# A block of sliding-window attention, mixer and MLP: modulation sums and the output projection's chain listed later, unit 0 packed over two queues, and a unit's products with V in one burst in place of two

## Chip, cores and metric

The kernel runs on one core of a Trainium2 chip. The metric is the device time of one execution in microseconds (us). Engines are named as in the profile: PE (TensorE, matmul), DVE (VectorE), ACT (ScalarE), POOL (GpSimd) and SP (SyncE, which here only issues DMAs).

## The reference

One batch of S = 2048 rows, D = 576 columns, H = 32 heads of 18, a window of W = 256, all in float32:

```python
mod = (_silu(c) @ w_mod).reshape(c.shape[0], 6, 1, -1)       # sa, ca, ga, sb, cb, gb
h = _layernorm(x) * (1 + ca) + sa
x = x + ga * _A_ref(h, A_wqkv, A_wo)      # attention: causal, 256 keys per query, then @ wo
h = _layernorm(x) * (1 + cb) + sb
x = x + gb * _B_ref(h, B_w1, B_w2, B_w3, B_w4)
# _B_ref: x1 = x + shift(gelu(ln(x) @ w1)) @ w2;  x1 + gelu(ln(x1) @ w3) @ w4   (w3: 576 x 4608)
```

## The kernel before

Each float32 operand of a matmul is split in a high and a low part, and products are taken from both, so one product of the reference is two or three matmuls. Phase A does the first layer norm, the projections to q, k and v, the attention, and most of the output projection; phase B/C does the mixer and the MLP, with weights and rows that flow through PE without a list.

**Attention.** It is cut in 32 units (c, g, hq): four chunks c of eight heads, four groups g of 512 rows, two halves hq of four heads. Names of tiles carry these numbers: `X0_3_0_1_2` is c 0, g 3, hq 0, bank 1 (of 128 query rows' windows), head 2. A unit's steps are:

- `uload` (L444 to L460): twelve DMAs on SP copy the q and k parts of the unit from DRAM (`qkh`, `qkl`) into the tile `U`, of which there are four.
- `s2` (L464 to L503): 16 score matmuls `sc` on PE (L477, three PSUM buffers), each reduced to a row maximum by DVE (L484). Then DVE negates and splits the maxima into `mr` (L490, L491), PE transposes them (`mT`, L498), ACT copies them out as `ms` (L500) and sends them by a DMA from its own queue (L501) into two rows of `U`, so that the next matmuls subtract the maximum by themselves.
- `s3` (L505 to L581): matmuls `X` (L526), which need those two rows, with a mask added by PE (L527, three PSUM buffers), exponential on ACT into `P` (L533, four buffers of four heads), and the products of P with V, `av` (L548): matmuls of 128 x 32 columns, four heads side by side in the PE array. They come in bursts: banks 0 and 3 in a burst in mid-unit, banks 1 and 2 in a burst at the unit's end. Then `fin1` copies the sums out on ACT (L553), `fin2` transposes and divides them (`oT`, L560, L562, `o`, L566), and `fin3` stores `o` from SP (`od`, L570) when hq is 1.

The X of a unit run 1.5 unit-times behind its scores, so that X of one unit and scores of the next but one alternate on PE. 

**Order.** Phase A's steps are put in a list `ev` of (time, step), with one unit per unit-time, and `play` (L40) calls them in the order of time. PE, POOL and SP keep that order (`manual`, L1192); DVE and ACT get theirs from the scheduler. An engine executes its instructions in order, so an instruction that waits holds up all behind it. SP's transfers also take turns on eight completion lanes, with ACT's: a transfer waits until the one before it on its lane has landed.

**Modulation vectors.** `modvec(v)` (L186 to L221) makes one of the vectors 2 to 5 beside the attention: five loads of rows of `w_mod` on SP (L196), products and sums on POOL (L205, L207, L208), then `spill`: PE adds over partitions with a matrix of ones (`pm`, L215), DVE reads it back (L216), and SP stores the vector (L219). L719 to L724 give these steps their times: `t0 = shift + 7.0 + 2.8 * n`, loads at `t0 + 0.35 * k`, spill at `t0 + 2.2`, store at `t0 + 2.35`.

**Output projection.** `s4(g, i)` (L736 to L785) handles one of 16 tiles of 128 rows: SP loads the tile of `o` back (`or`, L743) and the rows of x (L745); PE transposes it and ACT and DVE split it (`oTT`, L64 to L74); two halves of 14 matmuls each give `po` (L763), DVE adds x (L764), SP stores it (L769), and DVE makes the two layer norms that follow, whose results SP stores too. Times within a tile come from `d4` (load, transpose, half 0, half 1, norm, norm), and tiles of groups 0 to 2 are placed in the attention of the last chunk; group 3's follow it in phase B/C.

Of the kernel before, what the change touches and what calls it, by code (L numbers as in the profile page):

```python
# [19 lines left out]
P = 128  # L20
# [5 lines left out]
DH = 18  # L26
CH = 8
NCH = H // CH
SCALE = DH ** -0.5
# [21 lines left out]
class Kern:  # L51
# [75 lines left out]
    def phase_a(self):  # L127
        nc = self.nc
# [10 lines left out]
        with ExitStack() as st:  # L139
            self.ps = self.pool(st, "psA", space=PSUM)  # L140
            wp = self.pool(st, "wA")
            rp, lp, row = self.rp, self.lp, self.row
            pp = self.pool(st, "pA")
            V = [wp.tile([P, H * VA + 13], F32, name=f"V{t}") for t in range(NT)]
# [285 lines left out]
            def ualloc(n):  # L430
                def f():
                    pool, tag, nb = (lp, "L", 4) if n < 3 else (pp, "W", 1)
                    u = pool.tile([P, 4 * 512 + 2 * 768], F32R, tag=tag, name=f"U{n}", bufs=nb)
                    q = u[:, 0:2048].rearrange("p (q n) -> p q n", q=4)
                    k = u[:, 2048:].rearrange("p (j n) -> p j n", j=2)
                    nc.gpsimd.memset(k.bitcast(F32), 1.0)
                    nc.gpsimd.memset(q.bitcast(F32), 0.0)
                    units.append((q, k))
                return f

# [3 lines left out]
            def uload(c, g, hq):  # L444
                def f():
                    q, k = unit(c, g, hq)
                    h0 = 8 * c + 4 * hq

                    def put(dst, row, src, first, r, c0, c1):
                        v = src[first:first + 4 * DH, c0:c1].rearrange("(j r d) n -> d j r n", r=2, d=DH)[:, :, r, :]  # L450
                        nc.sync.dma_start(dst[row:row + DH].bitcast(F32), v)

                    c0, c1 = max(0, g * 512 - 256), g * 512 + 512
                    kd = k[:, :, 768 - (c1 - c0):]
                    for r in range(2):
                        for n, src in enumerate((qkl, qkh, qkh)):
                            put(kd, 64 * r + n * DH, src, D + h0 * DH, r, c0, c1)
                        for n, src in enumerate((qkh, qkh, qkl)):
                            put(q[:, r::2, :], 64 * r + n * DH, src, h0 * DH, r, g * 512, c1)
                return f  # L460

            KR = P - 2
# [42 lines left out]
            def s3(c, g, hq):  # L505
                QZ, KZ = unit(c, g, hq)
                Pb, Xb, abox = {}, {}, []
                banks = [0, 3, 1, 2] if g else [3, 1, 2]

                def sc(b, q):  # L510
                    def f():
                        if q == 0:
                            Pb[b] = pp.tile([P, 4, 3 * P], F32, tag="P", name=f"P{c}_{g}_{hq}_{b}", bufs=self.b_p)
                        j = q // 2
                        X = self.ps.tile([P, 3, P], F32, tag="st", name=f"X{c}_{g}_{hq}_{b}_{q}", bufs=self.b_st)
                        if b == 0:
                            mms = [(0, 1, 0, 0), (1, 2, 1, 0)]
                            mk = maskb[:, 1, :].unsqueeze(1).to_broadcast([P, 2, P])
                        elif b < 3:
                            mms = [(0, 3, b + 1, b - 1)]  # L520
                            mk = maskb
                        else:
                            mms = [(0, 2, 4, 2), (2, 1, 5, 3)]
                            mk = maskb[:, 0, :].unsqueeze(1).to_broadcast([P, 2, P])
                        for n, (x0, nb, kb, qb) in enumerate(mms):
                            nc.tensor.matmul(X[:, x0:x0 + nb, :].rearrange("p a b -> p (a b)"), KZ[:, j, kb * P:(kb + 1) * P], QZ[:, q, qb * P:(qb + nb) * P], start=(n == 0), stop=False)  # L526
                        nc.tensor.matmul(X[:, 0::2, :], self.identb, mk, start=False, stop=True)  # L527
                        Xb[b, q] = X
                    return f

                def expo(b, q):
                    def f():
                        nc.scalar.activation(Pb[b][:, q, :], Xb[b, q].rearrange("p a b -> p (a b)"), AF.Exp, scale=SCALE)  # L533
                    return f

                def av(b):
                    def f():
                        if not abox:
                            abox.append(self.ps.tile([P, 512], F32, tag="av", name=f"av{c}_{g}_{hq}", bufs=self.b_av))
                        first = b == banks[0]  # L540
                        segs = {0: [(-1, 0, 2 * P, P), (-2, 0, P, 0)],
                                1: [(0, 0, 3 * P, 0)] if g else [(0, 0, 2 * P, 0), (0, 2 * P, P, 2 * P)],
                                2: [(1, P, 3 * P, 0)],
                                3: [(2, 2 * P, 2 * P, 0), (3, 3 * P, P, 2 * P)]}[b]
                        for n, (kb, q0, w, p0) in enumerate(segs):
                            for q in range(4):
                                hv = (8 * c + 4 * hq + q) * VA
                                nc.tensor.matmul(abox[0][32 * q:32 * q + 32, q0:q0 + w], V[4 * g + kb][:, hv:hv + 32], Pb[b][:, q, p0:p0 + w], start=(first and n == 0), stop=(b == banks[-1]))  # L548
                    return f

                def fin1():
# [20 lines left out]
                steps = []  # L572
                n = 0
                for k, b in enumerate(banks):
                    for q in range(4):
                        steps += [(n, sc(b, q)), (n + self.l_e, expo(b, q))]
                        n += 1
                    if (len(banks) - k) % 2:
                        for b2 in banks[max(0, k - 1):k + 1]:
                            steps.append((n + self.l_av + (1 if k < len(banks) - 1 else 0), av(b2)))  # L580
                return steps, n, fin1, fin2, fin3  # L581

            Wo = {}
# [116 lines left out]
            for c in range(NCH):  # L700
                for g in range(NGA):
# [6 lines left out]
                        ev.append((tb + self.o3 - 0.001, lambda c=c, g=g, hq=hq, tb=tb + self.o3: sub3(c, g, hq, tb)))  # L708
                    if c == NCH - 1:
                        for i in range(4 if g < 3 else 0):  # L710
                            t4 = 2 * u + shift + 1.2 + self.o3 + self.ww + self.l_av / 16 + self.l_f + self.l_o + 0.5 * i - self.d4[0]
                            ev += [(t4 + d, f) for d, f in s4(g, i)]
                    u += 1
            uw = 2 * (3 * NGA) - 0.6 + shift
# [506 lines left out]
```

## Time and profile before

| what | value |
|---|---|
| median of 3 runs | 1826.36 us (1824.28 to 1827.94) |
| profiled execution | 1828.56 us |
| its span | 1826.5 us |
| mean granted clock of PE | 0.98 |
| attention, from the first scores to the last product with V | 196.0 to 714.6 us |
| tiles 0 to 11 of the output projection | from 580 us, between and behind the units |

The profile is of one execution. A row of its timeline has the start in us, the duration, engine, line, operation, output and inputs, and in brackets how long the engine was idle before it and on what it waited. The view of waits sums these brackets. PE's clock is given as a share of full speed.

### The profile page before, as it was taken

To read this page: it belongs to the slowest core of one execution; us is meant where nothing else is said; L and a number is where in the kernel's file an instruction comes from. 1 tells how busy PE (TensorE), PEld (TensorE's weight loads), DVE (VectorE), ACT (ScalarE), POOL (GpSimd) and SP (SyncE) were. 2 spreads that over 40 slices of the span, in tenths; PEclk is the share of its full clock that TensorE was granted. 3 is DMA by queue.
4 is the path that set the end of the run, shared out by engine and by line. 5 is a ranking of instruction groups with operands and counts; after the bars stand their busy time and mean duration, and the time that the engine had idled before them with its cause. 6 is when DMAs were issued, how large, how long until landed. Compare 5 with 4: busy or idle time off the path is not lost.

```text
span 1826.5 us, 30141 instructions
## 1 busy us (share of the span) xinstructions
PE 1742.4 (95%) x11700; PEld 1508.4 (83%) x11700; DVE 981.2 (54%) x2673; ACT 595.1 (33%) x1262; POOL 388.7 (21%) x380
## 2 busy tenths in 40 slices
PE   8999899898997798999899999999999999999999
PEld 5898667566775676999899999999999999999998
DVE  5302377676876687887744444444444434444433
ACT  4622166455664334444221111112111112111111
POOL 5501201221030111111323332333322111111100
PEclk8999999999999998999999999999999999999999
DMA  6424544444353546742311110111111000000002
GB/s 178 122 92 167 170 115 127 117 119 106 105 147 106 147 135 202 223 153 67 101 35 54 40 54 28 54 54 49 40 34 35 15 27 28 28 28 28 1 1 104
DMA packets 97711, 156.88 MB, mean 86 GB/s; under 512 B 11034, under 2 KB 40478, under 8 KB 97570
## 3 DMA queue, kind: packets, MB, share of 16 engines
q1 hardware_dynamic: 86882, 135.56, 25.1%
q10 hardware_dynamic: 10688, 19.40, 3.0%
q8 instruction: 92, 1.51, 0.4%
q14 instruction: 49, 0.40, 0.1%
HBM read 107.06 MB, written 47.20 MB: 84 GB/s over the span
## 4 chain that ended last, share of the span: by engine, by line
PE 58%; DVE 3%; DMA 1%; issue 1%; ACT 0%; POOL 0%; SPq 0%; DVEq 0%; ACTq 0%; POOLq 0%
PE p L1147 25%; PE p L1118 21%; PE pg L959 2%; PE w L1012 2%; PE p L1120 2%; PE p L1119 2%; PE po L763 2%; DMA rw<-in_B_w_dram 1%; PE av L548 0%; PE X L526 0%; DVE xr L99 0%; SPq L848 0%; DVE G L977 0%; DVE x L1013 0%; ACT G L976 0%
## 5 line engine op out<-in xcount | busy, mean ns | idle before, releaser
L1147 PEld LDWEIGHTS p<-CW,Gc 128*128 128x128 f32 x3456 | 474.9, 189 | 16.1 <-DVE Gc L1129 3.7
L1147 PE MATMUL p<-CW,Gc 128*128 128x288 f32 x3456 | 483.3, 296 | 3.4 <-DVE Gc L1129 3.4
L1118 PE MATMUL p<-LNT,CW 128*128 128x512 f32 x1728 | 419.3, 392 | 0.0
L1118 PEld LDWEIGHTS p<-LNT,CW 128*128 128x128 f32 x1728 | 316.8, 188 | 58.4
L1126 ACT ACTIVATE gfc<-p 128x512 f32<-128x512 f32 x144 | 86.1, 598 | 735.7 <-PE p L1120 735.7
L1151 DVE TENSOR_TENSOR acc<-p,acc 128x288 f32<-128x288 f32 x340 | 153.6, 455 | 318.2 <-PE p L1147 314.9
L484 DVE CUSTOM_DVE_ANT_0 sc<-sc,mask 128x384 f32<-128x384 f32 (+2 forms) x512 | 262.3, 554 | 104.0 <-PE sc L477 101.1
L533 ACT ACTIVATE P<-X 128x384 f32<-128x384 f32 x480 | 223.2, 490 | 154.2 <-PE X L527 141.5
L477 PE MATMUL sc<-U 126*128 126x384 f32 (+2 forms) x512 | 202.6, 414 | 8.4 <-DVE m L484 3.6
L526 PE MATMUL X<-U 128*128 128x384 f32 (+2 forms) x704 | 184.4, 320 | 4.9 <-ACT P L533 2.2
L526 PEld LDWEIGHTS X<-U 128*128 128x128 f32 x704 | 129.3, 195 | 37.1 <-issue 27.7
L1151 DVE TENSOR_TENSOR accw<-p,accw 128x288 f32<-128x288 f32 x204 | 90.0, 453 | 129.7 <-PE p L1147 128.1
L527 PE MATMUL X<-maskb,identb 128*128 128x256 bf16 x480 | 138.6, 289 | 0.0
L1129 DVE TENSOR_TENSOR Gc<-gfc,Gc 128x512 fp32r<-128x512 f32 x144 | 125.9, 875 | 4.5
L422 PE MATMUL pq<-hT,Wq 128*128 128x512 f32 x504 | 121.9, 400 | 2.3 <-POOL Wq L380 1.6
L422 PEld LDWEIGHTS pq<-hT,Wq 128*128 128x128 f32 x504 | 95.3, 191 | 24.4 <-POOL Wq L380 1.9
L477 PEld LDWEIGHTS sc<-U 126*128 126x128 f32 x512 | 101.5, 204 | 15.6 <-DVE m L484 8.5
L1098 POOL TENSOR_TENSOR CW<-r,CW 128x1024 fp32r<-128x1024 f32 x17 | 41.3, 2427 | 282.5 <-DVE CW L1096 282.5
L548 PE MATMUL av<-P,V 128*32 128x256 f32 (+2 forms) x1472 | 93.5, 386 | 0.0
L1128 ACT CAST Gc<-gfc 128x512 fp32r<-128x512 f32 x144 | 89.4, 621 | 4.6
L1102 POOL TENSOR_TENSOR CW<-r,CW 128x1152 fp32r<-128x1152 f32 x17 | 46.3, 2725 | 158.4 <-DVE CW L1101 158.4
L527 PEld LDWEIGHTS <-identb 128*128 128x128 bf16 x480 | 46.8, 97 | 37.6 <-issue 21.0
(1055 smaller groups left out, 1977.4 us busy)
## 6 DMA issues: line engine op xcount, KB each, us to landing
U<-qkh SPq DMA_DIRECT2D x160, 72.0 KB
U<-qkh SPq DMA_DIRECT2D x96, 108.0 KB
r<-in_B_w_dram SPq DMA_DIRECT2D x18, 576.0 KB
qkh<-hl ACTq DMA_DIRECT2D x36, 256.0 KB
qkl<-hl ACTq DMA_DIRECT2D x36, 256.0 KB
r<-in_B_w_dram SPq DMA_DIRECT2D x18, 512.0 KB
U<-qkl SPq DMA_DIRECT2D x80, 72.0 KB
U<-qkl SPq DMA_DIRECT2D x48, 108.0 KB
```

Of the source, the lines that this page charges most:

```text
L422: nc.tensor.matmul(pq, a, b, start=(n == 0), stop=(n == len(pl) - 1))
L477: nc.tensor.matmul(sc[:, lo:], QZ[:KR, q, i * P:(i + 1) * P], KZ[:KR, j, i * P + lo:(i + 3) * P], start=True, stop=True)
L484: nc.vector.tensor_tensor_reduce(out=sc[:, lo:], in0=sc[:, lo:], in1=mask[:, lo:], scale=1.0, scalar=-3e38, op0=ALU.add, op1=ALU.max, accu ...
L526: nc.tensor.matmul(X[:, x0:x0 + nb, :].rearrange("p a b -> p (a b)"), KZ[:, j, kb * P:(kb + 1) * P], QZ[:, q, qb * P:(qb + nb) * P], start ...
L527: nc.tensor.matmul(X[:, 0::2, :], self.identb, mk, start=False, stop=True)
L533: nc.scalar.activation(Pb[b][:, q, :], Xb[b, q].rearrange("p a b -> p (a b)"), AF.Exp, scale=SCALE)
L548: nc.tensor.matmul(abox[0][32 * q:32 * q + 32, q0:q0 + w], V[4 * g + kb][:, hv:hv + 32], Pb[b][:, q, p0:p0 + w], start=(first and n == 0), ...
L1118: nc.tensor.matmul(pg, W3[:, ws, fs], L[:, xs, :], start=(i == 0), stop=False)
L1128: nc.scalar.copy(Gh, gf)
L1129: nc.vector.tensor_tensor(out=Gl, in0=gf, in1=Gh.bitcast(F32), op=ALU.subtract)
L1147: nc.tensor.matmul(po, a, w, start=(i == 0), stop=(i == len(seq) - 1))
L1151: nc.vector.tensor_tensor(out=acc[t][:, cs], in0=po, in1=acc[t][:, cs], op=ALU.add)
```

## The change

Four parts. (1) The modulation vectors start at `shift + 5.0 + 4.2 * n`, and their spill and store come 3.7 and 3.9 unit-times later. (2) The chain of the output projection for groups 0 to 2 is listed `l_r = 0.4` later, with the two halves and first norm a little later still. (3) Unit 0's q stack is cleared on DVE, and its six q loads are issued from ACT's queue. (4) All four banks' products with V are one burst, listed 0.6 of a step after the unit's last X; bank 0's P, which now waits longest, has four tiles of its own from another pool.

```diff
-                    nc.gpsimd.memset(q.bitcast(F32), 0.0)
+                    (nc.vector if n == 0 else nc.gpsimd).memset(q.bitcast(F32), 0.0)
...
-                            put(q[:, r::2, :], 64 * r + n * DH, src, h0 * DH, r, g * 512, c1)
+                            put(q[:, r::2, :], 64 * r + n * DH, src, h0 * DH, r, g * 512, c1, nc.scalar if c == g == hq == 0 else nc.sync)
...
-                        if q == 0:
-                            Pb[b] = pp.tile([P, 4, 3 * P], F32, tag="P", name=f"P{c}_{g}_{hq}_{b}", bufs=self.b_p)
+                        if b == 0:
+                            Pb[b, q] = lp.tile([P, 3 * P], F32, tag="Wc", name=f"P{c}_{g}_{hq}_{b}_{q}", bufs=6)
+                        else:
+                            if q == 0:
+                                Pb[b] = pp.tile([P, 4, 3 * P], F32, tag="P", name=f"P{c}_{g}_{hq}_{b}", bufs=self.b_p)
+                            Pb[b, q] = Pb[b][:, q, :]
...
-                    if (len(banks) - k) % 2:
-                        for b2 in banks[max(0, k - 1):k + 1]:
-                            steps.append((n + self.l_av + (1 if k < len(banks) - 1 else 0), av(b2)))
+                for b in banks:
+                    steps.append((n + 0.6, av(b)))
...
-                            t4 = 2 * u + shift + 1.2 + self.o3 + self.ww + self.l_av / 16 + self.l_f + self.l_o + 0.5 * i - self.d4[0]
+                            t4 = 2 * u + shift + 1.2 + self.o3 + self.ww + self.l_av / 16 + self.l_f + self.l_o + self.l_r + 0.5 * i - self.d4[0]
...
-                t0 = shift + 7.0 + 2.8 * n
+                t0 = shift + 5.0 + 4.2 * n
...
-                ev += [(t0 + 2.2, spill), (t0 + 2.35, store)]
+                ev += [(t0 + 3.7, spill), (t0 + 3.9, store)]
...
-    d4 = (-0.2, 0.1, 0.3, 0.5, 0.8, 1.2)
+    d4 = (-0.2, 0.1, 0.38, 0.56, 0.85, 1.2)
+    l_r = 0.4
```

The rows below are the order of instructions in the two programs; lines of the changed kernel are four higher from L526 to L570 and three higher from L743 on. **The end of a steady unit on PE**, before (unit 0_2_1 ends, 0_3_0 begins; scores are of 0_3_1):

```order
L526 MATMUL X0_2_1_2_3_3198<-U1_1945 128x384
L527 LDWEIGHTS identb_78
L527 MATMUL X0_2_1_2_3_3198<-maskb_166,identb_78 128x2x128
L477 MATMUL sc0_3_1_2_0_3202<-U3_2171 128x384
L548 MATMUL av0_2_1_3126<-P0_2_1_1_3113,V8_157 32x384 x4
L548 MATMUL av0_2_1_3126<-P0_2_1_2_3173,V9_158 32x384 x4
L526 MATMUL X0_3_0_0_0_3214<-U2_2061 128x128
L526 MATMUL X0_3_0_0_0_3214<-U2_2061 128x256
L527 LDWEIGHTS identb_78
L527 MATMUL X0_3_0_0_0_3214<-maskb_166,identb_78 128x2x128
```

And after, same place:

```order
L530 MATMUL X0_2_1_2_3_3207<-U1_1945 128x384
L531 LDWEIGHTS identb_78
L531 MATMUL X0_2_1_2_3_3207<-maskb_166,identb_78 128x2x128
L477 MATMUL sc0_3_1_2_0_3211<-U3_2171 128x384
L530 MATMUL X0_3_0_0_0_3215<-U2_2061 128x128
L530 MATMUL X0_3_0_0_0_3215<-U2_2061 128x256
L531 LDWEIGHTS identb_78
L531 MATMUL X0_3_0_0_0_3215<-maskb_166,identb_78 128x2x128
L477 MATMUL sc0_3_1_2_1_3220<-U3_2171 128x384
L552 MATMUL av0_2_1_3222<-P0_2_1_0_0_3025,V7_156 32x256
L552 MATMUL av0_2_1_3222<-P0_2_1_0_1_3059,V7_156 32x256
L552 MATMUL av0_2_1_3222<-P0_2_1_0_2_3068,V7_156 32x256
```

The next unit's first X stands behind the second burst before, and ahead of the single burst after; of that burst the first three of 24 instructions are shown, and the rest of bank 0 and banks 3, 1 and 2 follow them. Nothing of the burst is left in mid-unit.

**The first tile of the output projection on PE**, before: `mT3_1_1` is the transpose of a unit's maxima, and `oTT0pa` needs the tile that SP loads back.

```order
L498 MATMUL mT3_1_1_7010<-identr_76,mr3_1_1_6976 8x128 x4
L477 MATMUL sc3_2_0_0_3_7018<-U0_1870 128x384
L526 MATMUL X3_1_0_1_3_7020<-U2_2061 128x384
L527 LDWEIGHTS identb_78
L527 MATMUL X3_1_0_1_3_7020<-maskb_166,identb_78 128x2x128
L68 MATMUL oTT0pa_7026<-ident_71,or0_6958 128x128 x4
L72 MATMUL oTT0pb_7033<-ident_71,or0_6958 64x128
L477 MATMUL sc3_2_0_1_0_7037<-U0_1870 128x384
L526 MATMUL X3_1_0_2_0_7041<-U2_2061 128x384
```

After, around the same transpose:

```order
L552 MATMUL av3_1_0_7105<-P3_1_0_3_6981,V6_155 32x256 x4
L552 MATMUL av3_1_0_7105<-P3_1_0_3_6981,V7_156 32x128 x4
L552 MATMUL av3_1_0_7105<-P3_1_0_1_7021,V4_153 32x384 x4
L552 MATMUL av3_1_0_7105<-P3_1_0_2_7064,V5_154 32x384 x4
L530 MATMUL X3_1_1_0_1_7132<-U3_2171 128x128
L530 MATMUL X3_1_1_0_1_7132<-U3_2171 128x256
L531 LDWEIGHTS identb_78
L531 MATMUL X3_1_1_0_1_7132<-maskb_166,identb_78 128x2x128
L477 MATMUL sc3_2_0_2_2_7137<-U0_1870 128x384
L68 MATMUL oTT0pa_7141<-ident_71,or0_7076 128x128 x4
L72 MATMUL oTT0pb_7148<-ident_71,or0_7076 64x128
L530 MATMUL X3_1_1_0_2_7153<-U3_2171 128x128
```

Before, two X and one score matmul lie around it behind `mT3_1_1`; after, `oTT0pa` has moved behind the rest of that unit, the next unit's first X and the whole burst.

**The loads of modulation vector 2 on SP**, before: `modd2` is the store, listed 0.15 behind the sum on PE.

```order
L196 DMA wm2_3_3315<-in_w_mod_dram 128x576
L196 DMA wm2_4_3387<-in_w_mod_dram 64x576
L451 DMA U2_2061<-qkl_139 18x2x768
L451 DMA U2_2061<-qkh_138 18x2x768 x2
L451 DMA U2_2061<-qkh_138 18x2x512 x2
L451 DMA U2_2061<-qkl_139 18x2x512
L451 DMA U2_2061<-qkl_139 18x2x768
L451 DMA U2_2061<-qkh_138 18x2x768 x2
L451 DMA U2_2061<-qkh_138 18x2x512 x2
L451 DMA U2_2061<-qkl_139 18x2x512
L219 DMA modd2_134<-wm2_0_3111 1x576
```

After:

```order
L196 DMA wm2_3_2956<-in_w_mod_dram 128x576
L196 DMA wm2_4_3011<-in_w_mod_dram 64x576
L451 DMA U0_1870<-qkl_139 18x2x512
L451 DMA U0_1870<-qkh_138 18x2x512 x4
L451 DMA U0_1870<-qkl_139 18x2x512 x2
L451 DMA U0_1870<-qkh_138 18x2x512 x4
L451 DMA U0_1870<-qkl_139 18x2x512
L451 DMA U1_1945<-qkl_139 18x2x512
L451 DMA U1_1945<-qkh_138 18x2x512 x4
L451 DMA U1_1945<-qkl_139 18x2x512 x2
L451 DMA U1_1945<-qkh_138 18x2x512 x4
L451 DMA U1_1945<-qkl_139 18x2x512
```

Before, one unit's twelve loads lie between the last row of `w_mod` and the store; after, those of three units and a store of `o` do, of which the first two units' are shown.

More of the change, by code (lines that the diff above doesn't have):

```diff
@@ L447, in f, with put @@
                     h0 = 8 * c + 4 * hq
-                    def put(dst, row, src, first, r, c0, c1):
+                    def put(dst, row, src, first, r, c0, c1, eng=nc.sync):
                         v = src[first:first + 4 * DH, c0:c1].rearrange("(j r d) n -> d j r n", r=2, d=DH)[:, :, r, :]
-                        nc.sync.dma_start(dst[row:row + DH].bitcast(F32), v)
+                        eng.dma_start(dst[row:row + DH].bitcast(F32), v)
                     c0, c1 = max(0, g * 512 - 256), g * 512 + 512
@@ L532, in f @@
                     def f():
-                        nc.scalar.activation(Pb[b][:, q, :], Xb[b, q].rearrange("p a b -> p (a b)"), AF.Exp, scale=SCALE)
+                        nc.scalar.activation(Pb[b, q], Xb[b, q].rearrange("p a b -> p (a b)"), AF.Exp, scale=SCALE)
                     return f
@@ L547, in f @@
                                 hv = (8 * c + 4 * hq + q) * VA
-                                nc.tensor.matmul(abox[0][32 * q:32 * q + 32, q0:q0 + w], V[4 * g + kb][:, hv:hv + 32], Pb[b][:, q, p0:p0 + w], start=(first and n == 0), stop=(b == banks[-1]))
+                                nc.tensor.matmul(abox[0][32 * q:32 * q + 32, q0:q0 + w], V[4 * g + kb][:, hv:hv + 32], Pb[b, q][:, p0:p0 + w], start=(first and n == 0), stop=(b == banks[-1]))
                     return f
```

## The prediction

> **What bounds the kernel now.** I read the page first, then what the tensor engine (PE) waited for, then its timeline and granted clock where it waits.
>
> ```profile
> span 1826.5 us, 30141 instructions
> PE 1742.4 (95%) x11700; PEld 1508.4 (83%) x11700; DVE 981.2 (54%) x2673; ACT 595.1 (33%) x1262; POOL 388.7 (21%) x380
> ```
>
> PE is busy for 95% of the span, so the time can fall only where PE waits (84 us), where it is busy at a low clock, or where its own work shrinks. The change adds no arithmetic. So I ask which waits it touches. The view of waits gives releaser, us in total, times, longest:
>
> ```profile
> PE pm L215 <- POOL wm L208: 17.9, 4, 6.1
> PE oTT0pa L68 <- DMA or<-od: 8.4, 1, 8.4
> PE oTT4pa L68 <- DMA or<-od: 6.4, 1, 6.4
> PE po L763 <- DVE oT L70: 4.8, 3, 2.1
> PE sc L477 <- DMA U<-qkl: 3.6, 2, 3.0
> PE X L526 <- DMA U<-ms: 2.0, 2, 1.5
> ```
>
> The first four lines are the modulation sums and the chain ahead of the output projection: 37.5 us that listing steps later can reach. A wait costs more than itself, as windows of PE time right behind the waits show (the columns after the width are PE, weight loads, DVE, ACT and Pool with their counts, then the granted clock, the DMA share and GB/s):
>
> ```profile
> 238.90:242.90 4.00, 3.96 (x40) 3.46 (x41) 3.16 (x13) 2.45 (x5) 0.00 (x0) 1.00 0.45 125
> 320.10:325.10 5.00, 4.99 (x24) 3.52 (x28) 3.03 (x11) 1.86 (x4) 0.00 (x0) 0.66 0.14 47
> 358.60:363.60 5.00, 5.00 (x41) 3.16 (x41) 2.06 (x6) 0.49 (x1) 0.00 (x0) 0.69 0.26 63
> 400.00:407.00 7.00, 6.93 (x43) 5.31 (x47) 3.65 (x12) 1.96 (x4) 0.76 (x2) 0.57 0.39 95
> 443.70:448.70 5.00, 4.96 (x24) 3.98 (x24) 2.90 (x9) 1.07 (x3) 0.00 (x0) 0.67 0.55 130
> 199.20:205.20 6.00, 5.75 (x20) 4.62 (x21) 1.33 (x8) 0.00 (x1) 0.00 (x0) 0.72 0.45 140
> 580.00:585.00 5.00, 4.95 (x23) 3.89 (x24) 3.06 (x10) 2.21 (x5) 0.00 (x0) 0.65 0.35 124
> 636.00:643.00 7.00, 7.00 (x32) 5.89 (x32) 4.46 (x13) 2.21 (x5) 0.00 (x0) 0.60 0.52 177
> 665.00:673.00 8.00, 7.80 (x50) 6.25 (x51) 4.70 (x15) 1.96 (x4) 0.79 (x2) 0.79 0.09 34
> 690.00:698.00 8.00, 7.82 (x42) 5.51 (x43) 4.24 (x18) 2.83 (x8) 0.79 (x2) 0.61 0.26 78
> ```
>
> Width times (1 - clock) is what each lost: at a clock of 0.66 over 5 us, 1.7 us of work that full speed would have saved. The first row is the counter-example to which I come back. **Modulation sums** (PE's timeline, with the wait in brackets):
>
> ```profile
> 320.11 1.75 PE L215 MATMUL pm<-wm,ones 128*128 128x288 f32 x4 [2.44 <-POOL wm L208]
> 358.60 2.29 PE L215 MATMUL pm<-wm,ones 128*128 128x288 f32 x4 [5.39 <-POOL wm L208]
> 400.07 2.29 PE L215 MATMUL pm<-wm,ones 128*128 128x288 f32 x4 [3.97 <-POOL wm L208]
> 443.74 2.29 PE L215 MATMUL pm<-wm,ones 128*128 128x288 f32 x4 [6.12 <-POOL wm L208]
> 309.96 1.03 SPq L196 DMA_DIRECT2D wm<-in_w_mod_dram  x2
> 302.73 1.51 PE L548 MATMUL av<-P,V 128*32 128x256 f32 x32
> 314.55 1.51 PE L548 MATMUL av<-P,V 128*32 128x256 f32 x32
> ```
>
> Waits 2.44 + 5.39 + 3.97 + 6.12 = 17.92; clock 5x0.34 + 5x0.31 + 7x0.43 + 5x0.33 = 7.9. Together 25.8. The first PE instruction came 10.2 us after SP issued the last loads (309.96 to 320.11). In that time the last two loads land and Pool multiplies and adds two more rows. The first bursts of two units in a row start at 302.73 and 314.55, so a unit, which is one unit-time of the list, takes 11.8 us. Before, the last load is listed 0.8 of a unit-time ahead of the sum (2.2 less 4x0.35), 9.4 us, which is less than 10.2. After, it is listed 2.3 ahead (3.7 less 1.4), 27 us. That leaves 17 us of slack over the 10.2, and 13 over the worst of the four, whose wait was 3.7 longer. I therefore take 25.3 of the 25.8 as saved. The four pairs of matmuls on PE stay, as do Pool's chunks, now spread over 3.7 unit-times in place of 2.2. What the loads pass on SP are loads of one unit and a store; the sum's own store moves behind more unit loads, and nobody reads the vectors before the output projection. Bounds: 17.9 if the clock drops for another reason, 25.8.
>
> On the clock, the row comes first: 2.44 us of wait was followed by 0.66 over 5 us, 1.54 us (at 238.94, below) by 1.00. The Trainium skill, "TensorE: Matmul & The Clock Gate", section "What's actually happening", says that the clock falls to half after at least one idle window of about 3.4 us. This trace disagrees, since a shorter wait sufficed. By the page's figure the waits of about 2 us that I leave standing below would cost no clock, and my sum would be 1.7 us lower for each.
>
> **One burst in place of two.** In the steady unit that begins above at 302.73 (first burst, banks 0 and 3), these rows of PE, its weight loads and ACT's and SP's queues follow; the last two are from other units:
>
> ```profile
> 304.16 0.19 PEld L526 LDWEIGHTS X<-U 128*128 128x128 f32 x1 [0.20 <-issue]
> 304.89 0.48 PE L498 MATMUL mT<-identr,mr 128*8 128x128 f32 x4
> 306.15 0.62 ACTq L501 DMA_DIRECT2D U<-ms  x1
> 308.03 1.50 PE L548 MATMUL av<-P,V 128*32 128x384 f32 x16
> 308.40 0.27 SPq L451 DMA_DIRECT2D U<-qkh  x1
> 309.46 0.50 PE L526 MATMUL X<-U 128*128 128x128 f32 x2
> 238.94 0.42 PE L526 MATMUL X<-U 128*128 128x256 f32 x2 [1.54 <-DMA U<-ms]
> 539.91 0.41 PE L526 MATMUL X<-U 128*128 128x256 f32 x2 [0.45 <-DMA U<-ms]
> ```
>
> Gain: the same matmuls run (32 and 16 in the trace), but PE changes between small tiles and the full array once less. The first burst lasts to 304.16 and ends with 0.20 of idle ahead of the next weights; one burst less a unit saves about that: 32 x 0.20 = 6.4. That bank 0's products are now kept in four tiles of their own costs nothing: ACT writes as many of the same size, and six buffers hold a unit's four and the next unit's first. Price: the next unit's first X needs the row of maxima that ACT sends at 306.15. That row is in at 308.40, 2.25 us behind the send: SP's load issued then shares a DMA lane with it and waits for its landing. Before, X came at 309.46, behind the second burst, with 1.06 to spare. After, this X is listed ahead of the burst, so PE reaches it where the burst began, at 308.03 less the change into small tiles, which I estimate at 0.1, half of the 0.20 on the way out. It waits 0.4 to 0.6; I take 0.55. Behind it on PE stand the burst, all X and the scores, so nothing fills the gap. Units 2 to 26 have this form, 25 x 0.55 = 13.8. The two that waited already (238.94, 539.91) wait one burst (1.43) longer, less the 0.55 counted for one of them: +2.3. From unit 27 on, output projection stands between. In all +16.1 - 6.4 = +9.7. Bounds: -6.4 (PE paced by its buffers there, so nothing is lost) and +14 (if the transposes mT, from which a burst of cover goes, also wait 0.15 for DVE).
>
> **Output projection.**
>
> ```profile
> 580.05 1.09 PE L68 MATMUL oTT0pa<-ident,or 128*128 128x128 f32 x4 [8.40 <-DMA or<-od]
> 635.99 1.09 PE L68 MATMUL oTT4pa<-ident,or 128*128 128x128 f32 x4 [6.39 <-DMA or<-od]
> 574.14 0.27 SPq L451 DMA_DIRECT2D U<-qkl  x1
> 574.51 0.39 SPq L570 DMA_DIRECT2D od<-o  x1
> 577.14 0.35 SPq L743 DMA_DIRECT2D or<-od  x1
> ```
>
> Tile 0's transpose waits for a chain on SP: store issued at 574.51, load back at 577.14, data at 580. The chain itself keeps its length. What changes is what PE does meanwhile: in the new order the rest of a unit stands ahead of the transpose, five X-and-score pairs more, one X of the next unit, the whole burst and one X. From rows above: mT to burst 3.1 (304.89 to 308.03, five pairs, so 0.6 each), a burst of twice 1.43, two more pairs 1.2, less the 0.9 of the pair and a half that it had: 6.3 us of cover. 8.4 - 6.3 leaves 2.1, and I keep a clock drop of 1.7: saving 8.40 + 1.75 - 3.8 = 6.3. Tile 4's wait of 6.39 is about as long as the same cover; I keep 1.5 for stores that now stand ahead of its load on SP and 0.8 of clock: 6.39 + 2.80 - 2.3 = 6.9. The two waits of about 2 for the split transposes (4.8 in three, the longest 2.1) get two more X pairs as cover; with clock 8x0.21 + 8x0.39 = 4.8, I take 5.5 of 8.9. Given back: tiles 10 and 11 now both run behind the last burst with nothing between, two waits of 2 and a clock drop, -5; and tile 1's load is queued on SP behind twelve loads of a unit, -1. Sum 12.7, taken as 12. Bounds: 20 (nothing kept, nothing given back) and -3 (the chain starts as much later as PE reaches it later, and the end is exposed).
>
> **Unit 0.**
>
> ```profile
> 189.07 7.17 SPq L451 DMA_DIRECT2D U<-qkh  x4
> 199.23 0.52 PE L477 MATMUL sc<-U 126*128 126x128 f32 x3 [3.00 <-DMA U<-qkl]
> ```
>
> SP issues four loads in 7.17 us, blocked. With six of twelve on ACT's queue the last is earlier; ACT's casts and stores behind them are later, and DVE takes two subtractions between the first two score reductions. Clearing the stacks on DVE in place of Pool lies under PE's projections, which run until the wait. At stake: 3.00 and 6x0.28 = 1.7 of clock. I take half, 2.5; bounds 4.7 and -2 (the loads as late as now, plus two subtractions). The Trainium skill, "DMA: Bandwidth & Descriptors", section "Issuing engines are not separate DMA queues", says that issuing from several engines saves only the time to issue. No run here splits the two. By it, six issues at the 0.27 of the row at 574.14 would save 1.6, and my sum would be 0.9 higher.
>
> **Sum.** The profiled execution took 1828.56 (1826.5 of span and 2.06 around it): 1828.56 - 25.3 + 9.7 - 12 - 2.5 = 1798.5. The median before, 1826.36, lies 2.2 lower, and so the forecast is **1796**.
>
> **Rivals**, all as medians. (a) The merged burst brings its gain and no wait: 1796 - 16 = 1780. For it: DVE and ACT are 54% and 33% busy, so X has room elsewhere; against it: the 1.06 to spare is less than the burst of 1.43. (b) The output projection keeps its waits since the chain only moves: 1796 + 12 = 1808, with the unit-0 loss of 2 at most 1813. For it: SP's store waits behind a unit load (574.14) whose lane is the row of maxima. (c) The change doesn't do what it says for the sums: Pool's chain still ends late, because SP reaches the loads later than listed; 1796 + 25 = 1821. Against it: for the first sum SP issued them 10.2 us ahead, where the list had 9.4. (d) Slower: the row of maxima lands late in every unit. The burst no longer covers it, and each microsecond costs 25. Other savings are 25.3 + 6.4 + 12 + 2.5 = 46.2, so it decides from 46.2 / 25 = 1.85 us of wait a unit, that is a transfer of some 3.6 in place of 2.25 us (308.40 - 307.93 is its wait at 2.25, and each microsecond more is one more). At the 2.0 which the unit at 539.91 would have (0.45 + 1.43 and the mode change), 25 x 2.0 - 46.2 = +4: 1830; with a clock drop after each it would pass 1860. For it: the two slow rows; against it: two in 32.
>
> **Chances.** Forecast 0.52, (a) 0.12, (b) 0.22, (c) 0.07, (d) 0.07. The forecast's own range is 1788 to 1804. The whole range takes in most of (a) and (b), 1781 to 1815. A measurement of this kernel tells about 0.2%, 3.7 us. Faster: forecast, (a), (b) and half of (c), 0.89; same 0.05; slower 0.06.
>
> **What would show it.** Sums: the wait pm for Pool is gone and the clock is 1.00 there. Burst: about 25 new waits of X for the row of maxima, 0.4 to 0.7 each, and one burst of 2.7 us a unit; no such waits is (a), waits of 2 are (d). Projection: tiles 0 and 4 wait 0 to 4 in place of 8.4 and 6.4, and po behind the last burst waits some 2 twice. Unit 0: the wait at 199 is 0 to 2. I'd be wrong if PE waits in a unit for DVE's maxima, because the first burst covered them, or if SP's lanes tie the store of o to something later.

## Result and profile after

The changed kernel takes 1828.63 us (median of 20 runs, 1821.72 to 1836.52), the kernel before 1827.53 (20 runs). The ratio is 1.0006 with an interval of 0.9993 to 1.0018: no difference, where 1796 was forecast. The profiled execution took 1828.71, span 1826.9.

The view of PE's waits of the changed kernel, beside the one shown of before:

```profile
PE mT L498 <- DVE o L570: 14.3, 11, 2.5
PE X L530 <- ACT P L537: 5.8, 13, 1.5
PE oTT11pa L68 <- DMA or<-od: 4.9, 1, 4.9
PE sc L477 <- DVE m L484: 4.3, 10, 1.2
PE oTT0pa L68 <- DMA or<-od: 3.7, 1, 3.7
PE X L530 <- DMA U<-ms: 3.7, 3, 2.5
```

The first and second line of before, the sums and tile 0's 8.4, are gone or halved, and tile 4's is gone. On top stands a wait that the same view of before has with 3.9 us: the transposes of the maxima, mT, wait for DVE's `o`.

```profile
PE mT L498 <- DVE o L566: 3.9, 3, 1.6
```

The row of maxima, for which some 25 waits of 0.55 were forecast, has three in this view. The view lists only time in which PE stands idle, though, and the run with the burst ahead, below, shows that the row held up the first X of 22 of the 25 steady units.

The sums and unit 0 went as forecast. The timeline of PE has the first sum without a wait, and windows behind the places of before's first two sums have the clock at 1.00:

```profile
315.99 1.14 PE L215 MATMUL pm<-wm,ones 128*128 128x288 f32 x4
320.00:330.00 10.00, 8.95 (x92) 6.11 (x92) 5.70 (x26) 5.88 (x15) 0.00 (x0) 1.00 0.30 91
358.60:363.60 5.00, 4.95 (x56) 3.27 (x58) 4.25 (x18) 3.03 (x7) 0.00 (x0) 1.00 0.29 87
```

Where the time went shows in marks along the attention. They are starts of PE instructions in the two traces, mT by the unit's number; "two bursts" is the changed kernel with the bursts of before, the first experiment below:

| mark, us | before | after | two bursts |
|---|---|---|---|
| mT of unit 0 | 220.4 | 217.4 | 218.1 |
| mT of unit 2 | 244.6 | 243.7 | 240.5 |
| mT of unit 27 | 570.6 | 565.6 | 539.1 |
| last product with V | 714.6 | 695.2 | 655.6 |
| last matmul of the program | 1822.5 | 1822.9 | 1781.2 |

After is 3 us ahead when the units begin, but gains only 2 more up to unit 27, although 25 us of sums fell away: two units take 24 to 28 us, mostly 25 to 26.6, where before they took 24 wherever no sum lay among them. A first reading of the two traces alone was that the end of the attention gives back the rest, since the last product with V comes 19.4 earlier and the program ends no earlier. The third column refutes it: there the last product comes 59 earlier and the program ends 41 earlier. Part of that lead is output projection that was only moved behind it, but a lead of the attention is kept.

One unit shows the new wait. These are rows of PE and DVE (start, duration) in the changed kernel, behind the first unit of a pair:

```profile
290.03 0.60 PE L564 MATMUL oT<-ident,avs 128*128 128x128 f32 x4
290.67 0.26 DVE L566 RECIPROCAL rc<-oT 128x16 f32<-128x16 f32 x1
290.85 0.57 DVE L484 CUSTOM_DVE_ANT_0 sc<-sc,mask 128x384 f32<-128x384 f32 x1
...
292.75 0.60 DVE L491 SCALAR_TENSOR_TENSOR mr<-m,mr 128x16 fp32r<-128x16 f32 x1
293.27 0.55 DVE L484 CUSTOM_DVE_ANT_0 sc<-sc,mask 128x384 f32<-128x384 f32 x1
293.75 0.59 DVE L484 CUSTOM_DVE_ANT_0 sc<-sc,mask 128x384 f32<-128x384 f32 x1
294.26 0.59 DVE L484 CUSTOM_DVE_ANT_0 sc<-sc,mask 128x384 f32<-128x384 f32 x1
294.78 0.45 DVE L570 TENSOR_TENSOR o<-oT,rc 128x288 f32<-128x288 f32 x1
295.28 0.41 PE L498 MATMUL mT<-identr,mr 128*8 128x128 f32 x4 [1.73 <-DVE o L570]
```

And such rows of the kernel before at the same unit:

```profile
290.79 1.51 PE L548 MATMUL av<-P,V 128*32 128x256 f32 x32
290.84 0.17 DVE L491 SCALAR_TENSOR_TENSOR mr<-m,mr 128x16 fp32r<-128x16 f32 x1
290.93 0.56 DVE L484 CUSTOM_DVE_ANT_0 sc<-sc,mask 128x384 f32<-128x384 f32 x1
291.41 0.60 DVE L484 CUSTOM_DVE_ANT_0 sc<-sc,mask 128x384 f32<-128x384 f32 x1
291.92 0.45 DVE L566 TENSOR_TENSOR o<-oT,rc 128x288 f32<-128x288 f32 x1
293.04 0.48 PE L498 MATMUL mT<-identr,mr 128*8 128x128 f32 x4
```

mT and oT share one buffer of PSUM (tag `tr`, one buffer), so mT cannot start until DVE has divided the sums of the unit before, `o`. In the first unit of most pairs DVE's order has, in both kernels, `o` far behind its reciprocal: behind three reductions, mr and two or three more reductions. There `o` is written into a tile whose store by SP belongs to the pair before. That the scheduler put it there because of this store is an inference; it fits the run with half tiles below, where `o` moves up. Before, PE ran the first burst (290.79 to 292.3) in this time, and `o` was ready at 292.4, ahead of mT. After, that burst is gone from mid-unit, PE arrives 1.73 early, and everything behind mT on PE stands.

### The profile page after: what moved, and what is told of

Same layout as the page of the kernel before. It is cut to its first block, busy times and chain, and to the rows that moved or that the text cites. A ratio compares the mean times of both kernels' runs of the same rounds, so it can differ in the third digit from the quotient of the medians.

```text
span 1826.9 us, 30134 instructions
## 1 busy us (share of the span) xinstructions
PE 1746.7 (96%) x11700; PEld 1509.4 (83%) x11700; DVE 982.7 (54%) x2674; ACT 598.9 (33%) x1262; POOL 389.6 (21%) x379
## 3 DMA queue, kind: packets, MB, share of 16 engines
q8 instruction: 92, 1.51, 0.3%
## 4 chain that ended last, share of the span: by engine, by line
PE 54%; DVE 2%; POOL 0%; issue 0%; DMA 0%; ACT 0%; SPq 0%; ACTq 0%; POOLq 0%
PE p L1150 25%; PE p L1121 21%; PE p L1123 2%; PE p L1122 2%; PE w L1015 2%; PE pg L962 2%; DVE x L1016 0%; DMA r<-in_B_w_dram 0%; DVE G L980 0%; POOL CW L1105 0%; DVE LNT L70 0%; DVE CW L1100 0%; DVE xm L889 0%; DVE G L967 0%; DVE Gc L1132 0%
## 5 line engine op out<-in xcount | busy, mean ns | idle before, releaser
L477 PEld LDWEIGHTS sc<-U 126*128 126x128 f32 x512 | 100.3, 200 | 18.7 <-DVE m L484 12.5
L552 PE MATMUL av<-P,V 128*32 128x256 f32 (+2 forms) x1472 | 86.1, 382 | 0.0
```

The costliest lines, as they stand in the source:

```text
L477: nc.tensor.matmul(sc[:, lo:], QZ[:KR, q, i * P:(i + 1) * P], KZ[:KR, j, i * P + lo:(i + 3) * P], start=True, stop=True)
```

## Experiments

The theories were: (1) a burst ahead of mT was cover, under which DVE finishes `o` and the maxima; (2) the prediction's, the next unit's first X ahead of the burst waits for the row of maxima; (3) a burst of 2.8 us is too long for what three buffers of PSUM give DVE and ACT to do; and later (4), a sharper form of (3): DVE falls behind between bursts and catches up in them, so the spacing of bursts counts. Each has the median of 4 to 12 runs beside the kernel before, whose median in the five sets was 1826.4, 1827.6, 1828.1, 1826.8 and 1827.8. Differences of under 3 us are not read. Each trace is of one execution, which can lie several us off the median (that of the run with both edits lies 8.6 above), so waits from traces show where time goes and only roughly how much of the median it is.

**Two bursts put back.**

```diff
-                for b in banks:
-                    steps.append((n + 0.6, av(b)))
+                    if (len(banks) - k) % 2:
+                        for b2 in banks[max(0, k - 1):k + 1]:
+                            steps.append((n + self.l_av + (1 if k < len(banks) - 1 else 0), av(b2)))
```

(and P in tiles of four heads for all banks)

> The changed kernel with the two bursts of before put back; sums, projection and unit 0 as changed. Theory 1 (the single burst costs some 24 us in the attention, since it uncovers DVE's division o behind which the transposes of the maxima wait): unit 27's transpose of maxima comes near 542 in place of 565.6, no wait of mT for o over 4 us in all, and the total is below the changed kernel by 10 to 24 (1805 to 1818), less whatever the end of the attention and the mixer give back. Theory 2 (the burst is worth about nothing, the loss lies behind the attention): unit 27 as in the changed kernel, total within 4 of it.

Measured: 1789.79, ratio 0.9806 (0.9792 to 0.9820). Unit 27's mT starts at 539.1. Its waits of mT for o:

```profile
PE mT L498 <- DVE o L566: 2.7, 3, 0.9
```

The single burst alone costs the whole gain: 1828.6 - 1789.8 = 38.8. That is more than the 24 at most which theory 1 had, so there is more in it than `o`.

**The sums alone, on the kernel before** (the hunk on `modvec` only).

> The kernel before with the modulation vectors' new times only. If a lead won in the attention is carried to the end: unit 27's transpose near 545 in place of 570.6, total 1828.5 less 25, 1801 to 1805. If the mixer behind gives back some 7 of any lead, because its order is fixed and waits for stores on SP: 1808 to 1812. If the waits for POOL return elsewhere: above 1820.

Measured: 1802.58, ratio 0.9874 (0.9858 to 0.9890), 23.8 below; unit 27's mT at 546.1. The lead of 24.5 there arrives at the end.

**The single burst alone, on the kernel before.**

> The kernel before with the single burst only. Theory 1: slower by 15 to 26 (1843 to 1854), with mT waiting for o some 14 us in all in about eleven units of the first half of a pair, and a pair of units taking 26 in place of 24 us. Theory 2 (the prediction's term, the row of maxima arriving 0.55 late): slower by about 10, with some 25 waits of X for the row and none of mT for o.

Measured: 1851.59, ratio 1.0152 (1.0133 to 1.0171), 25.2 slower.

```profile
PE mT L498 <- DVE o L570: 15.1, 11, 3.0
PE pm L215 <- POOL wm L208: 11.8, 4, 5.1
```

Theory 1's line is there with its count. The waits for the sums shrink from 17.9 to 11.8: part of the price lies in waits that were there anyway, so it is 25.2 here and 38.8 where those waits are gone. What else makes up the difference was not tried.

**`o` in half tiles, on the changed kernel.**

```diff
-                    if hq == 0:
-                        orow[c, g] = pp.tile([P, 4, 144], F32, tag="o", name=f"o{c}_{g}", bufs=self.b_o)
-                    o = orow[c, g]
+                    o = orow[c, g, hq] = pp.tile([P, 4, 72], F32, tag="o", name=f"o{c}_{g}_{hq}", bufs=2)
...
-                    if hq == 1:
-                        nc.sync.dma_start(self.od[g].rearrange("(t p) d -> p t d", p=P)[:, :, c * 144:(c + 1) * 144], orow[c, g])
+                    c0 = c * 144 + hq * 72
+                    nc.sync.dma_start(self.od[g].rearrange("(t p) d -> p t d", p=P)[:, :, c0:c0 + 72], orow[c, g, hq])
```

In DVE's order `o` now stands behind one reduction in every unit of the attention but the last two, in front of mr.

> The changed kernel with o in two half tiles, each stored behind its own unit, so that DVE can write o without waiting for a store of the unit just before, and its order puts o right behind the reciprocal. Sixteen more stores on SP. Theory 1: the waits of mT for o fall from 14.3 to under 3, the pairs of units come down from 26 towards 24.5 to 25, and the total falls by 6 to 14; waits of X for the row of maxima (0.4 to 0.6 each) appear where the others go. If o is not the cause: the total is within 3, or higher by the stores.

Measured: 1814.94, ratio 0.9942 (0.9929 to 0.9956), 13.7 below the changed kernel. The waits of mT for o are gone, and others stand in their place:

```profile
PE sc L477 <- DVE m L484: 5.7, 13, 2.1
PE mT L498 <- DVE mr L491: 5.3, 5, 2.1
PE X L530 <- ACT P L537: 4.9, 10, 1.5
...
PE X L530 <- DMA U<-ms: 4.1, 4, 1.9
```

So the late `o` is a cause and costs 13.7 of 38.8. In the view the row of maxima does not take its place at 25 units; waits for DVE's maxima and mr do. By the reading shown below with the burst ahead, though, the row holds up the first X here as it does in the changed kernel.

**The first of two bursts moved behind mT**, otherwise the two-burst kernel:

```diff
-                            steps.append((n + self.l_av + (1 if k < len(banks) - 1 else 0), av(b2)))
+                            steps.append((n + self.l_av + (3.5 if k < len(banks) - 1 else 0), av(b2)))
```

> The two-burst kernel (1789.8) with its first burst moved from just ahead of the transpose of the maxima mT to one X behind it; nothing else. Theory 1 (a burst ahead of mT is the cover under which DVE finishes the maxima and o): waits of mT for o and mr come back, 12 to 17 us in all, and the total rises by 8 to 14, to 1798 to 1804. Theory 3 (only the length of a burst matters, since DVE and ACT run dry behind three buffers of PSUM): within 3 of 1789.8.

Measured: 1805.94, ratio 0.9881 (0.9863 to 0.9900), 16.1 above the two-burst kernel, somewhat more than the 8 to 14 that theory 1 had.

```profile
PE mT L498 <- DVE o L566: 10.2, 11, 1.6
```

Nothing but the place of a short burst changed, and the eleven waits of mT are back. That the burst ahead of mT was cover is shown.

**The burst cut in two at the unit's end**, with `o` in half tiles (banks 0 and 3 at `n + 0.6`, banks 1 and 2 at `n + 2.6`).

> The changed kernel with o in half tiles (1814.9), and its single burst cut in two at the unit's end: banks 0 and 3 where the burst was, banks 1 and 2 two X-and-score pairs later. The cover ahead of mT stays away. Theory 3: the loss that half tiles left was from the burst's length of 2.8 us, so the total falls by 8 to 14 towards 1801 to 1807. Theory 1: the cover of mT is what counts, waits of mT for DVE stay as they were (some 5 for mr), the second change of mode costs up to 6, total 1812 to 1821.

Measured: 1815.84, ratio 0.9936 (0.9921 to 0.9950): as with the uncut burst, 1814.94. Theory 3 in this form falls: a burst of 2.8 us is not worse than two of 1.4 that stand close together.

**The single burst ahead of the next X**, on the changed kernel:

```diff
-                    steps.append((n + 0.6, av(b)))
+                    steps.append((n - 0.05, av(b)))
```

> The changed kernel with its single burst one X earlier, ahead of the next unit's first X as the second burst of before was. Theory 2 (the prediction's: that X waits for the row of maxima, the burst being behind it): the waits of X for the row and of X for ACT vanish and the total falls by 5 to 12. Theories 1 and 3: the transposes still wait for o some 14 us, the total is within 4 of 1828.6.

Measured: 1816.12, ratio 0.9930 (0.9909 to 0.9950), 12.5 below the changed kernel, though mT still waits for o as long:

```profile
PE mT L498 <- DVE o L570: 16.1, 11, 2.8
```

So the place behind the next X costs 12.5, and theory 2 is right about the place and about the row. The view hides it: in units 2 to 27 of the changed kernel it lists 1.2 us of waits for the row and 3.7 for ACT's P. But the landing of the row can be read from SP's next load on the same lane, as the prediction read it. In a steady unit of the changed kernel:

```profile
308.67 0.62 ACTq L501 DMA_DIRECT2D U<-ms  x1
310.63 0.42 PE L477 MATMUL sc<-U 126*128 126x384 f32 x1
310.91 0.27 SPq L451 DMA_DIRECT2D U<-qkl  x1
311.03 0.47 PE L530 MATMUL X<-U 128*128 128x128 f32 x2
```

The row is sent at 308.67 and the load issued at 310.91; X starts 0.12 behind it. In 22 of the 25 units from 2 to 26 it starts as close behind that load, as it did in the kernel before at 539.91, where the view does list a wait for the row. In the other units of the kernel before the first X starts 0.3 or more behind that load, and in this run 1.7 or more. From the start of the score ahead to the start of this X 0.51 us pass on average in the changed kernel; for other X behind a score the median is 0.26. That is some 6.3 us lost in 25 units, and by 6.5 the stretch of units 2 to 27 shrinks in this run. Half of it is no idle time: PE is on record as busy, with the score ahead, until X starts. Another 3.8 lies where the units begin: from mT of 0 to mT of 2 it takes 22.5 in place of 26.3, where the row of unit 1 was late by 2.47.

**Both, `o` in halves and the burst ahead.**

> The changed kernel with both: o in half tiles (which alone took 13.7 off it) and the single burst ahead of the next unit's first X (12.5 alone). If the late o and the row of maxima are two independent prices: 1800 to 1805, no waits of mT for o, none of X for the row. If they overlap: 1808 to 1813.

Measured: 1805.38, ratio 0.9871 (0.9854 to 0.9888). The two prices nearly add up: 23.2 together, 26.2 one by one. This kernel is still 15.6 above the two-burst one. mT waits for mr 6.8 in nine units.

**The same, and mT two pairs later** (`l_m` from 0.1 to 0.25).

> The kernel of e15 with the transposes of the maxima two X-and-score pairs later, so that DVE has the time that a burst of 1.4 us gave it, while the burst of 2.8 us behind them covers the row of maxima. If cover ahead of mT is all that the single burst still lacks: 1785 to 1793, the level of two bursts (1789.8) or up to 6 below, with waits of mT for mr under 1. If a long burst starves DVE and ACT: it stays at 1797 or above, with X and scores waiting for ACT and DVE.

Measured: 1803.44, ratio 0.9868 (0.9853 to 0.9884): the level of two bursts is not reached. The waits of mT for mr are gone, but scores wait for DVE (over the units 2 to 27 of each kernel, first this one, then two bursts):

```profile
PE sc L477 <- DVE m L484: 8.4, 19, 1.9
PE X L530 <- DMA U<-ms: 3.0, 2, 1.7
```

```profile
PE mT L498 <- DVE o L566: 2.7, 3, 0.9
PE mT L498 <- DVE mr L491: 0.6, 1, 0.6
PE X L526 <- DMA U<-ms: 0.3, 1, 0.3
```

Over units 2 to 27, DVE's own waits for scores, in the changed kernel and then in the two-burst kernel:

```profile
DVE sc L484 <- PE sc L477: 77.7, 56, 2.8
```

```profile
DVE sc L484 <- PE sc L477: 52.8, 65, 1.5
```

DVE's work is the same and the stretch of the changed kernel is 23.3 us longer, so that DVE is idle for 25 us more follows from that. What differs in kind is the single wait: up to 2.8 us behind single bursts, 1.5 behind two. Cover ahead of mT was not all: with mT late enough, PE waits at the next place at which it needs DVE, the scores. In that stretch the kernel is 7.1 us longer than with two bursts (305.7 against 298.6). Another 7.4 lies ahead of unit 2's mT (247.9 against 240.5), where mT is listed later in the first units too; a lower clock has a part in it (0.86 from mT of 0 to mT of 2, against 1.00).

**mr on POOL**, on the kernel of the run above: three small steps there in place of two on DVE.

> The kernel of e16 (one burst, o in halves, mT late, 1803.4) with the two small steps that make mr on POOL, three of them there: 0.35 us a unit off DVE. Theory 4: PE's waits of scores for DVE fall from 8.4 to 2 to 5, and the total by 3 to 8, to 1795 to 1800. If DVE's load is not what is left: within 2 of 1803.4, or above it where mr comes late from POOL.

Measured: 1826.10, ratio 0.9994 (0.9979 to 1.0009), 22.7 above.

```profile
PE mT L500 <- POOL mr L493: 24.7, 7, 5.1
```

This tells nothing of DVE: POOL's own queue has the rows of the modulation vectors, and later weights of the output projection, ahead of mr, and mT waited for POOL.

**The first burst behind mT, with `o` in half tiles.**

> The two-burst kernel with its first burst behind mT (1805.9), with o in half tiles. If the 16.1 that the move cost were all from o standing late in DVE's order: back to 1790 to 1794. If the cover ahead of mT is needed for the maxima too: 1796 to 1803, with waits of mT for mr of 3 to 6.

Measured: 1796.83, ratio 0.9836 (0.9816 to 0.9856). Of the 16.1 that the move cost, 9.1 go with an early `o`; 7.0 stay, with mT waiting for mr 2.4 and X for the row of maxima 4.3 in the whole span. So the cover was needed for more than `o`; the 2.4 for mr are less than the 3 to 6 expected, and how the 7.0 divide is open.

**More work for DVE, with two bursts and with one**: the two steps that make mr are done twice.

```diff
-                    nc.vector.tensor_scalar(mr[:, :, 0:4], m, -1.0, None, op0=ALU.mult)
-                    nc.vector.scalar_tensor_tensor(out=mr[:, :, 4:8], in0=m, scalar=-1.0, in1=mr[:, :, 0:4].bitcast(F32), op0=ALU.mult, op1=ALU.subtract)
+                    for _ in range(2):
+                        nc.vector.tensor_scalar(mr[:, :, 0:4], m, -1.0, None, op0=ALU.mult)
+                        nc.vector.scalar_tensor_tensor(out=mr[:, :, 4:8], in0=m, scalar=-1.0, in1=mr[:, :, 0:4].bitcast(F32), op0=ALU.mult, op1=ALU.subtract)
```

> The two-burst kernel (1789.8) with the two small steps on DVE that make mr done twice in each unit, 0.35 to 0.58 us more of DVE a unit. Theory 4: with a pause every half unit DVE catches up, so the total rises by 0 to 5. If DVE bounds the unit with two bursts as well: 9 to 18.

> The kernel of e16 (one burst, o in halves, mT late, 1803.4) with the same doubled steps. Theory 4: with one pause a unit DVE is late for the scores already (8.4 us of waits), so nearly all of the added DVE time shows: plus 8 to 16, with waits of scores for DVE of 15 or more. If DVE's load is not what is left in e16: plus 0 to 5, as with two bursts.

Measured: with two bursts 1797.73, ratio 0.9842 (0.9818 to 0.9866), 7.9 more; with one (the kernel with mT late) 1824.24, ratio 0.9979 (0.9963 to 0.9994), 20.8 more. In units 2 to 27 DVE got 13.7 and 17.2 us of work more. With one burst nearly as much shows as waits of scores, 24.4 in place of 8.4:

```profile
PE sc L477 <- DVE m L484: 24.4, 21, 3.4
```

Both went over what theory 4 had, 0 to 5 and 8 to 16. With two bursts the added work shows ahead of mT, where the doubled steps stand (waits of mT for o and mr 11.5 in place of 3.3), so there too DVE has little slack at that place. With one burst the clock adds to it: 0.96 in units 2 to 27, against 0.99 without the doubled steps. Span times (1 - clock), the median of each kernel's runs, is 36.4 against 27.0, so some 9 of the 20.8 may be clock. The direction is theory 4's, that one pause in a unit leaves DVE less slack than two; its size is not shown by this pair.

**Four bursts, one a bank**, on the two-burst kernel.

> The two-burst kernel (1789.8) with four bursts, one a bank, each a bank later than its X. The price of a burst's two changes of mode is read here: at the 0.20 of the prediction, 64 more bursts cost 12.8, so 1800 to 1804; if a boundary costs nothing, 1788 to 1792. By theory 4 (DVE falls behind while scores and X run and catches up while a burst runs, and three buffers of PSUM let it be some 1.5 us late) PE waits for DVE no more than in the two-burst kernel.

Measured: 1818.50, ratio 0.9953 (0.9937 to 0.9970), 28.7 above two bursts, 0.45 for each of 64 added bursts, where 0.20 for each would have been 12.8. mT waits for o 3.7, with two bursts 2.7. The bursts of one unit:

```profile
286.94 0.86 PE L548 MATMUL av<-P,V 128*32 128x256 f32 x16
289.90 0.86 PE L548 MATMUL av<-P,V 128*32 128x256 f32 x16
...
293.43 0.85 PE L548 MATMUL av<-P,V 128*32 128x384 f32 x8
295.85 1.31 PE L548 MATMUL av<-P,V 128*32 128x384 f32 x8
296.32 0.14 PEld L548 LDWEIGHTS av<-P,V 128*32 128x32 f32 x2 [0.32 <-ACT P L533]
```

They take 3.88 against 1.51 + 1.50 of two. 0.46 of the 0.87 is the last one: it stands right behind the X of its own bank and waits in its middle for ACT's last P, as its weight load shows. Without that a burst more costs 0.2, the value in the prediction; with it 0.45.

**The other parts alone, on the kernel before.**

> The kernel before with the output projection's new times only. With the two bursts, sums and projection together with unit 0 were worth 12.8 more than the sums alone, of which unit 0 some 3: so 1815 to 1820, with waits for the tiles 0 and 4 of 2 to 4 and 0 to 2.

Measured: 1818.81, ratio 0.9955 (0.9940 to 0.9971), 9.3 below.

> The kernel before with unit 0's loads over two queues only: 1822 to 1826, the wait of 3.0 for the loads at the first scores gone or under 1. If the queues share what limits them: within 1 of the kernel before.

Measured: 1821.23, ratio 0.9966 (0.9954 to 0.9977), 6.9 below and a little below the 1822 to 1826 expected; the waits for U's loads are gone from its view of waits.

**`o` in half tiles with two bursts**, to see whether more is to be had.

> The two-burst kernel (1789.8) with o in half tiles. Its waits of mT for o are 2.7 us, so at most that is to be had, against sixteen more stores on SP: 1786 to 1792.

Measured: 1790.41, ratio 0.9799 (0.9781 to 0.9817): nothing beyond the two-burst kernel, as expected where mT waits only 2.7 for `o`. These two are the fastest of those run, 37 us below the kernel before.

## Why the prediction was wrong

By its steps:

- **Sums**: right. 25.3 forecast, 23.8 measured alone.
- **Output projection**: right in kind, 12 forecast, 9.3 measured alone. Tile 0 keeps 3.7 where 2.1 was kept; tile 4's wait went; the exposed end came as one wait for tile 11's load (4.9) rather than two for its split, and tile 3's load, which the sum did not have, is waited for 2.9.
- **Unit 0**: right in sign, too small: 2.5 forecast with a bound of 4.7, 6.9 measured (4.2 to 8.4 by its interval). PE's first scores lose their wait, and unit 2 comes 4 earlier in that trace; the rest was not followed.
- The three together were forecast with 39.8, and the two-burst kernel has 36.6 of it. Of the rivals, (a), a merged burst without a wait, did not come, nor (b) and (c), by which projection or sums keep their waits, nor (d): the row of maxima was late by over 2 us in one unit only.
- **One burst in place of two**: wrong, and this alone moved the time out of the range. The step was "Bounds: -6.4 (PE paced by its buffers there, so nothing is lost) and +14 (if the transposes mT, from which a burst of cover goes, also wait 0.15 for DVE)". The net was put at +9.7 and is +38.8. The wait for the row came as forecast, in 22 of the 25 units, at half its size: 0.25 a unit on average in place of 0.55. What failed is the price of the lost cover. The prediction named the cover and the engine, also among the signs of being wrong, and priced it at 0.15 a unit without looking at what DVE had to do in that time. It counted the maxima alone, and not when the PSUM buffer of mT becomes free: that needs `o`, which stood behind mr and two reductions. The row at which this could be seen, DVE's `o` at 291.92 beside mT at 293.04, lay in the trace of before, 0.7 us from being late, and three such waits, 3.9 us in all, stood in its view.

What the runs put in its place, of 38.8: the late `o`, 13.7; the burst behind the next X, 12.5, which the prediction had with 16.1; and 12.6 that remain when these are subtracted one by one, 15.6 in the run without both. The traces show where it lies. The changed and the two-burst kernel are 41.7 apart at the last matmul: 3.2 ahead of unit 2's mT, 23.3 in units 2 to 27, 15.2 behind them. The 23.3 are nearly accounted for: 11.6 more waits of mT for o, 1.8 more for mr, 6.3 for the row, and up to 3.4 by a clock of 0.989 in place of 1.000. What lies behind them, where output projection and units alternate, was not separated.

A part of the price is not the waits themselves. By the span and clock that each run lists, span times (1 - clock) is 31.1 us in the changed kernel and 21.5 in the two-burst one (medians), so by this estimate up to 10 of the 38.8 were lost to a lower clock, less what fell into PE's waits. The run with mT late, with 27.0, has up to 5 of its 13.6 above two bursts from it. How much of the rest there is DVE's lack of slack was not separated. The gain of one burst less, 6.4 in the prediction, lies inside these numbers; adding bursts gave 0.2 to 0.45 for each.

## To carry to other kernels

A stretch in which PE runs something that the other engines need not serve is not only its own cost: it is the time in which they catch up. Before such a stretch is moved or merged, list what each other engine finishes under it, by end times in the trace, and for the next PE instruction check every buffer that it reuses, not only its inputs. A short view of waits is no proof that nothing waits: compare the start of the instruction with the time at which its input landed. When several edits are made together, a change of zero may be three gains and a loss; each alone, or one put back, tells in one run.

## What the runs showed of the hardware

- The clock fell after a wait for tile 0 of 3.7 us as after before's 8.4: 0.65 over 580 to 585 in both traces. Keeping a part of a wait may keep all of the clock's loss:

```profile
580.00:585.00 5.00, 5.00 (x29) 5.00 (x29) 3.88 (x14) 1.97 (x4) 0.00 (x0) 0.65 0.81 160
```

- PE's busy time is not the work of PE alone: for the same matmuls it was 293.4, 294.0 and 298.5 us in units 2 to 27 of the two-burst kernel, the one with the burst ahead, and the changed one. Waits that the view doesn't list can be inside it: at 310.63 above, the score is on record as busy for 0.42 us, past the landing of the row for which PE's next matmul waits.
